# One joint turn of k and q, with k's remainder made in PSUM

## The chip, the cores and the metric

The kernel runs on one core of a Trainium2 chip. The metric is the device time of one execution in microseconds (us), as the median of several runs. The engines are TensorE (PE, with its weight loads as PEld), VectorE (DVE), ScalarE (ACT), GpSimd (POOL), and SyncE (SP), which issues all the transfers (DMA) of this program. Each engine works through its own instructions strictly in order and waits where one of them needs another engine's result.

## The reference

Attention over 8 batches, 12 heads, 448 tokens and 64 features, with q and k normalised by their root mean square; its output, 3584 rows of 768, goes through a feed-forward layer with w_in (768 x 2048), a squared ReLU scaled by s and shifted by b, and w_out (2048 x 768).

```python
def rmsnorm(x, g):
    rms = np.sqrt(np.mean(x * x, axis=-1, keepdims=True) + 1e-06)
    return x / rms * g
q_n, k_n = (rmsnorm(q, g_q), rmsnorm(k, g_k))
scores = scale * np.matmul(q_n, k_n.transpose(0, 1, 3, 2))
scores = scores - np.max(scores, axis=-1, keepdims=True)
attn = np.exp(scores)
attn = attn / (np.sum(attn, axis=-1, keepdims=True) + 1e-09)
out = np.matmul(attn, v)
...
h = x @ w_in
g = s * np.maximum(h, 0.0) ** 2 + b
return g @ w_out
```

## The kernel before

The 96 heads are worked on as 48 pairs, six pairs to a batch. The program is a list of slots, eight to a pair (four for each head j of the pair p), 384 in all, with a lead-in from slot -22 on. Nothing reorders the work: the loop writes each engine's instructions in the order of the slots, and `jobs` is a table that says which step is written in which slot. A step moved by one slot is moved past all that the slot holds, on each engine that it uses. In what follows a slot begins where its first product `st` (L451) begins.

In a slot s, PE computes a chunk of the transposed scores (`score_t`, L451 and L454), whatever is turned in this slot, a chunk of plain scores for a later pair (`score(s + AHEAD)`, L410), and the product with v of two slots earlier (`weigh`, L513). From slot 56 on six products of the feed-forward layer of the batch before are laid between these (`filler`, `ffn_in`, L208). DVE takes the maximum of the plain scores (`maximum`, L421); four of these make a row that a transfer puts beside q (`shift`). ACT takes the exponent (`exponent`).

All products are of two parts, so that they are exact enough: a value is rounded to a `hi` part, and what is left is the `lo` part. For a head of the first nine pairs (`NR`) the rows of k and q come as they lie in memory (`load_rows`), are normalised (`norm_rows`: ACT squares, DVE sums, POOL takes the power and multiplies), are turned by PE against the identity (`turn`, L278), and are split (`split_turned`): ACT rounds k and q out of PSUM (L286, L287, and q a second time into the other half of the partitions, L289), DVE makes the lo parts (L290 for k, L293 for q). `ka` holds k hi over k lo, `qa` q hi twice, `qb` q lo, and `kb` a copy of k hi that a transfer makes (`double_kb`, L398). Later pairs come turned from the host and use `norm`, `keep`, `spread`, `scale` and `split_kq`.

The weights w_in are 64-bit numbers in memory. They come in 24 pieces (`load_piece`, `convert`, L130 to L151), numbered 0 to 23 here: for each four instructions on DVE (L135, L138, L140, L143), two on ACT, and last one on POOL (L151), which writes the lo part `wil`. `PACE` says in which slots a piece begins; its hi part is written three slots later and its lo part four slots later. Block fc of the feed-forward layer needs pieces 6 * (fc // 4) to 6 * (fc // 4) + 5, in this order; block 12, the first that needs piece 23, is laid in slots 92 to 94. PSUM has eight banks, which a list hands out in turn (`psum`, `free`): a product waits until the bank that it is given has been read.

Of the kernel before, what the change touches and what calls it, by code (L numbers as in the profile page):

```python
# [9 lines left out]
F32 = mybir.dt.float32  # L10
# [17 lines left out]
AHEAD = 10  # L28
# [5 lines left out]
PACE = (-15, -10, *range(1, 61, 5), *range(59, 89, 3))  # L34
# [5 lines left out]
OUT = (92, *range(110, 141, 6), *(48 * b + i for b in range(3, 8) for i in range(14, 43, 7)))  # L40
# [3 lines left out]
def attention_then_relu2_ffn(  # L44
# [67 lines left out]
    warm = cpool.tile([P, 1], F32, name="warm")  # L112

# [128 lines left out]
    if True:  # L242
# [30 lines left out]
        def turn(p, j):  # L273
            raw = raws.pop((p, j))
            for t in range(2):
                tk, bank = psum(f"tk{p}_{j}_{t}")
                for c in range(NQ):
                    T.transpose(  # L278
                        tk[:D, c * QC : (c + 1) * QC], raw[:, t, c], ident[:QC, :QC]
                    )  # L280
                tks[p, j, t] = tk[:D, :SEQ], bank

        def split_turned(p, j):
            n, a = p % 2, slice(j * SEQ, (j + 1) * SEQ)
            (k, k_bank), (q, q_bank) = (tks.pop((p, j, t)) for t in range(2))
            S.copy(ka[n][:D, a], k)  # L286
            S.activation(qa[n][:D, a], q, AF.Copy, scale=gqk[:D])  # L287
            yield
            S.activation(qa[n][D:, a], q, AF.Copy, scale=gqk[:D])  # L289
            V.tensor_tensor(ka[n][D:, a], k, ka[n][:D, a].bitcast(F32), ALU.subtract)  # L290
# [364 lines left out]
        for p in range(NPAIR):  # L655
            s0 = W * p
            if p >= NR:
                at(s0 - 32, load, p)
                at(s0 - 28, norm, p)
                at(s0 - 24, keep, p)  # L660
            for j in range(2):
# [12 lines left out]
                at(s1 - 6, shift, p, j)  # L674
# [394 lines left out]
```

## Time and profile before

| | us |
|---|---|
| median of 3 runs | 1400.15 |
| lowest and highest run | 1399.1, 1400.77 |
| the profiled execution | 1402.48 |
| its span, from the first to the last instruction | 1400.7 |
| busy PE, DVE, ACT, POOL in it | 1379.6, 1038.5, 868.8, 1021.7 |
| start of slot 0, 56, 64 and 94 in the span | 24.22, 121.26, 144.56, 220.12 |

The page gives busy time by engine, the chain of waits, and groups of equal instructions with the mean time of one and the idle time of the engine ahead of them. "<-DVE nmx L421" names what ended the idle time. Since matmuls are pipelined, the time of one (0.37 us for the products of 448 columns) is longer than the distance from one to the next (0.2 us), so a busy PE may hide short waits; the distance between starts in the timeline is the better measure, and it is used throughout.

### The profile page before, as it was taken

What the parts mean: (1) busy time and instruction counts of PE and PEld (TensorE: products, weight loads), DVE (VectorE), ACT (ScalarE), POOL (GpSimd) and SP (SyncE); (2) the same over time, 40 slices, a digit from 0 to 9 for tenths busy, and PEclk for the clock granted to TensorE, in tenths of its full rate; (3) what the DMA queues carried; (4) which work ended last, traced back from release to release, by engine and by line L of the source; (5) the groups of instructions that cost most, each with busy time, mean ns of one, the idle gap of its engine ahead of it and who ended that gap; (6) DMA issues with size and microseconds to landing.
All of it is one profiled execution on the core that took longest, in us unless ns stands there. A gap on an engine that the chain in (4) does not pass through costs nothing. (4 is left out here: it accounts for less than half of the span.)

```text
span 1400.7 us, 22180 instructions
## 1 busy us (share of the span) xinstructions
PE 1379.6 (98%) x6976; PEld 1262.0 (90%) x6976; DVE 1038.5 (74%) x1603; ACT 868.8 (62%) x1658; POOL 1021.7 (73%) x940
## 2 busy tenths in 40 slices
PE   7999999999999999999999999999999999999998
PEld 5666888999999899999989989989999999999998
DVE  8999786888888778788788778565766665666655
ACT  5776666777777776776777777654544444444443
POOL 7687788777877787777787776267767777577763
PEclk8999999999999999999999999999999999999999
DMA  5566886777677677677677766354434333233331
GB/s 148 133 174 175 258 242 192 220 239 226 190 238 217 200 235 218 189 228 239 198 219 214 225 188 204 94 160 150 118 91 121 99 99 98 84 120 98 98 97 62
DMA packets 209253, 237.95 MB, mean 170 GB/s; under 512 B 72848, under 2 KB 187024, under 8 KB 209136
## 3 DMA queue, kind: packets, MB, share of 16 engines
q1 hardware_dynamic: 209136, 236.54, 57.6%
q8 instruction: 55, 0.90, 0.3%
q14 instruction: 62, 0.51, 0.1%
HBM read 178.00 MB, written 47.11 MB: 161 GB/s over the span
## 5 line engine op out<-in xcount | busy, mean ns | idle before, releaser
L208 PE MATMUL ph<-x,wih 128*128 128x448 f32 x1536 | 491.7, 366 | 0.5 <-DVE x L563 0.5
L848 PE MATMUL m<-t,gh 128*128 128x384 f32 x1568 | 399.3, 335 | 0.2
L208 PEld LDWEIGHTS ph<-x,wih 128*128 128x128 f32 x1536 | 288.6, 188 | 30.8 <-issue 6.7
L421 DVE TENSOR_REDUCE nmx<-sh 112x1 fp32r<-112x448 f32 x384 | 236.6, 618 | 85.3 <-PE sh L410 82.5
L208 PE MATMUL ph<-x,wil 128*128 128x448 f32 x768 | 294.0, 383 | 0.0
L848 PEld LDWEIGHTS m<-t,gh 128*128 128x128 f32 x1568 | 283.4, 188 | 1.0 <-DVE ot L863 0.9
L470 ACT ACTIVATE st<-st 128x448 f32<-128x448 f32 (+1 forms) x294 | 154.2, 524 | 192.9 <-PE st L454 189.9
L848 PE MATMUL m<-t,gl 128*128 128x384 f32 x784 | 262.6, 335 | 0.3 <-DVE gl L830 0.3
L829 ACT CAST gh<-g 128x896 fp32r<-128x896 f32 x112 | 105.4, 942 | 178.2 <-POOL g L819 178.2
L830 DVE TENSOR_TENSOR gl<-g,gh 128x896 fp32r<-128x896 f32 x112 | 127.7, 1141 | 107.2 <-ACT gh L829 107.2
L815 POOL TENSOR_TENSOR g<-g 128x256 f32<-128x256 f32 x112 | 94.6, 845 | 113.5 <-DVE g L814 113.5
L513 PE MATMUL av<-ah,vs 128*128 128x448 f32 x576 | 164.9, 367 | 0.8 <-DVE al L491 0.5
L451 PE MATMUL st<-qa,ka 128*128 128x448 f32 (+1 forms) x384 | 159.1, 414 | 4.1 <-DVE nmx L421 4.0
L208 PEld LDWEIGHTS ph<-x,wil 128*128 128x128 f32 x768 | 144.3, 188 | 17.9 <-issue 6.7
L478 ACT CAST ah<-st 128x448 fp32r<-128x448 f32 (+1 forms) x294 | 156.8, 533 | 1.3
L555 POOL TENSOR_TENSOR u<-uz,zb 64x448 f32<-64x448 f32 x96 | 126.7, 1320 | 42.1 <-DMA zb<-z_d 38.3
L410 PE MATMUL sh<-ka,qa 128*112 128x448 f32 x384 | 145.5, 382 | 3.6 <-DVE ka L290 1.8
L848 PEld LDWEIGHTS m<-t,gl 128*128 128x128 f32 x784 | 147.1, 188 | 0.6 <-DVE gl L830 0.6
L491 DVE TENSOR_TENSOR al<-st,ah 128x448 fp32r<-128x448 f32 x216 | 132.7, 614 | 18.7 <-ACT ah L478 15.8
L454 PE MATMUL st<-qb,kb 128*128 128x448 f32 (+1 forms) x384 | 140.4, 366 | 0.0
L394 POOL TENSOR_TENSOR ka<-kq,ka 64x448 fp32r<-64x448 f32 x78 | 95.5, 1224 | 57.0 <-ACT ka L391 52.3
L819 POOL TENSOR_TENSOR g<-g 128x256 f32<-128x256 f32 x112 | 125.9, 1124 | 0.0
(93 smaller groups left out, 2398.2 us busy)
## 6 DMA issues: line engine op xcount, KB each, us to landing
kq<-in_dram SPq DMA_DIRECT2D x78, 448.0 KB, 4.9
rb<-i_d SPq DMA_DIRECT2D x78, 448.0 KB, 5.9
r_d<-r SPq DMA_DIRECT2D x128, 224.0 KB, 3.1
raw<-in_dram SPq DMA_DIRECT2D x39, 448.0 KB, 5.1
raw<-r_d SPq DMA_DIRECT2D x64, 256.0 KB, 2.8
w64i<-in_dram SPq DMA_DIRECT2D x24, 512.0 KB, 4.7
w64o<-in_dram SPq DMA_DIRECT2D x32, 384.0 KB, 4.6
kb<-ka SPq DMA_DIRECT2D x96, 112.0 KB, 3.3
```

Of the source, the lines that this page charges most:

```text
L208: T.matmul(ph[:, :SEQ], w[:, cc, f0 : f0 + P], xs[b, cc][:, part, :], start=n == 0, stop=n == 3 * NCC - 1,)
L410: T.matmul(sh[:QC, :SEQ], qa[p % 2][:, a].rearrange("k (p c) -> k c p", c=NQ)[:, c], ka[p % 2][:, a], start=True, stop=True,)
L421: V.tensor_reduce(out=nmxs[p][:, c : c + 1], in_=sh[:QC, :SEQ], op=ALU.max, axis=AX.X, negate=True)
L451: T.matmul(st[:rows, :SEQ], ka[n][:, keys], qa[n][:, q], start=True, stop=False)
L454: T.matmul(st[:rows, :SEQ], kb[n][:, keys], qb[n][:, q], start=False, stop=True,)
L470: S.activation(st[:rows, :SEQ], st[:rows, :SEQ], AF.Exp)
L478: S.copy(ah[:rows], sts[i][0][:rows, :SEQ])
L491: V.tensor_tensor(al, st[:rows, :SEQ], ah[:rows].bitcast(F32), ALU.subtract)
L513: T.matmul(av[:, :SEQ], x, a, start=kc == 0 and m == 0, stop=kc == 3 and m == len(todo) - 1,)
L555: G.tensor_tensor(u[a], uzs.pop((p, j))[a], zb[a], ALU.mult)
L830: V.tensor_tensor(gl, g9[:, 1:8], gh.bitcast(F32), ALU.subtract)
L848: T.matmul(to, g[:, sa], w, start=m == 0 and n == 0, stop=m == NM - 1 and n == 2,)
```

## The change

`rows0` is laid so that k and q of a token lie side by side, and `turn` makes four turns of 128 columns (64 of k, 64 of q) into one PSUM bank where eight turns of 64 columns went into two. k comes out on partitions 0 to 63 and q on 64 to 127. From there `split_turned` differs by pair:

- q hi is written once by ACT, on partitions 64 to 127; its second copy is still written by ACT for pair 0, and by a transfer within SBUF (`move`) from pair 1 on.
- k lo is still made by DVE for pairs 0 and 1. From pair 2 on PE adds -k hi on the turned k: a product of `ka` with the constant `less`, a negative identity in its first 64 rows and columns and zero elsewhere, accumulated into the same bank; ACT then copies k lo out of PSUM a slot later.

With it go other numbers of the table: `AHEAD` is 9 (it was 10) and `shift` a slot later; `norm_rows` two slots earlier from pair 2 on; the last steps of the division (`invert`, `divide`) one or two slots later in batch 0, and `split_x` of its last pair one; `load` of pair 9 ten slots earlier; and `PACE`: piece 13 begins in slot 60 and no longer in 56, and the last, piece 23, in 90 and no longer in 86.

```diff
-AHEAD = 10
+AHEAD = 9
-PACE = (-15, -10, *range(1, 61, 5), *range(59, 89, 3))
+PACE = (-15, -10, *range(1, 56, 5), *range(60, 91, 3))
-OUT = (92, *range(110, 141, 6), ...
+OUT = (100, *range(110, 141, 6), ...
+    less = cpool.tile([P, P], F32R, name="less")
+    G.memset(less.bitcast(F32), 0.0)
+    S.activation(less[: P // 2, : P // 2], ident[: P // 2, : P // 2], AF.Copy, scale=-1.0)
...
         def turn(p, j):
             raw = raws.pop((p, j))
-            for t in range(2):
-                tk, bank = psum(f"tk{p}_{j}_{t}")
-                for c in range(NQ):
-                    T.transpose(
-                        tk[:D, c * QC : (c + 1) * QC], raw[:, t, c], ident[:QC, :QC]
-                    )
-                tks[p, j, t] = tk[:D, :SEQ], bank
+            tk, bank = psum(f"tk{p}_{j}")
+            for c in range(NQ):
+                T.matmul(
+                    tk[:, c * QC : (c + 1) * QC],
+                    raw[:, c].rearrange("p t d -> p (t d)"),
+                    ident[:QC, :QC],
+                    start=c == 0, stop=p < 2 and c == NQ - 1, is_transpose=True,
+                    skip_group_check=True,
+                )
+            tks[p, j] = tk, bank
 
         def split_turned(p, j):
             n, a = p % 2, slice(j * SEQ, (j + 1) * SEQ)
-            (k, k_bank), (q, q_bank) = (tks.pop((p, j, t)) for t in range(2))
+            tk, bank = tks.pop((p, j))
+            k, q = tk[:D, :SEQ], tk[D:, :SEQ]
             S.copy(ka[n][:D, a], k)
-            S.activation(qa[n][:D, a], q, AF.Copy, scale=gqk[:D])
+            S.activation(qa[n][D:, a], q, AF.Copy, scale=gqk[D:])
             yield
-            S.activation(qa[n][D:, a], q, AF.Copy, scale=gqk[:D])
-            V.tensor_tensor(ka[n][D:, a], k, ka[n][:D, a].bitcast(F32), ALU.subtract)
-            free.append(k_bank)
+            if p == 0:
+                S.activation(qa[n][:D, a], q, AF.Copy, scale=gqk[D:])
+            else:
+                move(qa[n][:D, a], qa[n][D:, a])
+            if p < 2:
+                V.tensor_tensor(ka[n][D:, a], k, ka[n][:D, a].bitcast(F32), ALU.subtract)
+            else:
+                T.matmul(
+                    tk[:, :SEQ], less, ka[n][:, a], start=False, stop=True, skip_group_check=True
+                )
             yield
+            if p >= 2:
+                S.copy(ka[n][D:, a], k)
             V.scalar_tensor_tensor(
...
-                at(s0 - 32, load, p)
+                at(s0 - (42 if p == NR else 32), load, p)
...
-                    at(s1 - 21, norm_rows, p, j)
+                    at(s1 - (21 if p < 2 else 23), norm_rows, p, j)
...
-                at(s1 - 6, shift, p, j)
+                at(s1 - 5, shift, p, j)
...
-            at(s0 + 13, invert, p)
-            at(s0 + 14, divide, p, 1)
-            at(s0 + 16, divide, p, 2)
-            at(s0 + 18, divide, p, 3)
+            first = p < NP
+            at(s0 + 13 + first, invert, p)
+            at(s0 + 14 + first, divide, p, 1)
+            at(s0 + 16 + first, divide, p, 2)
+            at(s0 + 18 + first + (p < NP - 1), divide, p, 3)
```

**PE, slots 10 to 12.** The turn of pair 3, head 0, in the kernel before (`sh` are the plain scores, `st` the transposed ones, `av` the product with v; four turns stand in a row that ends with x4).

```order
L451 MATMUL st10_613<-qa1_201,ka1_199 128x448
L454 MATMUL st10_613<-qb1_205,kb1_203 128x448
L278 MATMUL tk3_0_0_622<-ident_66,rows3_0_389 64x112 x4
L278 MATMUL tk3_0_1_627<-ident_66,rows3_0_389 64x112 x4
L410 MATMUL sh20_632<-ka0_198,qa0_200 112x448
L513 MATMUL av1_0_636<-e8_582,vf1_486 128x448
```

The same place in the changed kernel:

```order
L467 MATMUL st10_587<-qa1_204,ka1_202 128x448
L470 MATMUL st10_587<-qb1_208,kb1_206 128x448
L280 MATMUL tk3_0_597<-ident_66,rows3_0_378 128x112 x4
L426 MATMUL sh19_602<-ka0_201,qa0_203 112x448
L529 MATMUL av1_0_606<-e8_559,vf1_469 128x448
L467 MATMUL st11_608<-qa1_204,ka1_202 128x448
L470 MATMUL st11_608<-qb1_208,kb1_206 128x448
L426 MATMUL sh20_626<-ka0_201,qa0_203 112x448
L529 MATMUL av1_0_606<-e9_574,vf1_469 128x448
L467 MATMUL st12_634<-qa1_204,ka1_202 128x448
L470 MATMUL st12_634<-qb1_208,kb1_206 128x448
L303 MATMUL tk3_0_597<-ka1_202,less_74 128x448
```

Four turns have gone, and two slots later one product of 448 columns (L303) has come, which needs ACT's copy of k hi in `ka1`.

**SP, lead-in.** The transfers around the first `shift` (`qb0<-nmx0`) in the kernel before; `vf0` are the rows of v, `kb` the copies of k hi.

```order
L398 DMA qb0_204<-nmx0_321 1x112x4
L398 DMA kb0_202<-ka0_198 64x448
L324 DMA vf0_373<-in_3_dram 128x4x64 x2
L255 DMA rows3_0_389<-in_2_dram 112x512
L398 DMA qb0_204<-nmx0_321 1x112x4
```

The same place in the changed kernel:

```order
L414 DMA qb0_207<-nmx0_322 1x112x4
L340 DMA vf0_366<-in_3_dram 128x4x64 x2
L414 DMA qa1_204<-qa1_204 64x448
L258 DMA rows3_0_378<-in_2_dram 112x512
L414 DMA kb1_206<-ka1_202 64x448
L414 DMA qb0_207<-nmx0_322 1x112x4
```

The second copy of q hi (`qa1<-qa1`) now stands behind the shift and both loads of v; PE's plain score `sh8`, which stands ahead of the first `st0`, needs it.

**POOL, slots 91 to 94.** The end of the conversion of w_in (`wil3` is the last quarter of the lo part, `wai23` piece 23; `ri15` is the power of pair 15's norm, `vs0` a split of v), in the kernel before.

```order
L151 TENSOR_TENSOR wil3_1937<-wai23_2506,wih3_1936 128x512
L332 TENSOR_TENSOR v_rest_195<-vf11_2350,v_rest_195 128x2x64
L394 TENSOR_TENSOR ka1_199<-kq13_0_2408,ka1_199 64x448
L395 TENSOR_TENSOR qb1_205<-kq13_0_2408,qa1_201 64x448
L339 MEMSET vs0_2617 128x4x64 x2
L342 TENSOR_TENSOR vs0_2617<-vr12_2469,vs0_2617 128x4x2x64
L373 TENSOR_TENSOR kq13_1_2521<-kq13_1_2521,rb13_1_2523 128x448
L356 TENSOR_SCALAR ri15_2647<-ssq15_2614 128x14
L357 TENSOR_TENSOR ri15_2647<-ri15_2647,mhalf_71 128x14
L394 TENSOR_TENSOR ka1_199<-kq13_1_2521,ka1_199 64x448
```

The same place in the changed kernel:

```order
L410 TENSOR_TENSOR ka1_202<-kq13_0_2319,ka1_202 64x448
L411 TENSOR_TENSOR qb1_208<-kq13_0_2319,qa1_204 64x448
L355 MEMSET vs0_2535 128x4x64 x2
L358 TENSOR_TENSOR vs0_2535<-vr12_2376,vs0_2535 128x4x2x64
L389 TENSOR_TENSOR kq13_1_2432<-kq13_1_2432,rb13_1_2434 128x448
L372 TENSOR_SCALAR ri15_2565<-ssq15_2532 128x14
L373 TENSOR_TENSOR ri15_2565<-ri15_2565,mhalf_71 128x14
L154 TENSOR_TENSOR wil3_1960<-wai23_2520,wih3_1959 128x512
L410 TENSOR_TENSOR ka1_202<-kq13_1_2432,ka1_202 64x448
```

The lo part of piece 23 has moved from ahead of the split of v to behind pair 15's norm.

More of the change, by code (lines that the diff above doesn't have):

```diff
@@ L26 @@
 LAST = 15
-AHEAD = 10
+AHEAD = 9
 FIRST = -22
 FILL = (2, 2, 2)
-PACE = (-15, -10, *range(1, 61, 5), *range(59, 89, 3))
+PACE = (-15, -10, *range(1, 56, 5), *range(60, 91, 3))
 GAP = 2
 STEPS = {0: 2, 1: 3, 2: 4, 3: 5, 5: 6, 6: 7, 8: 8, 9: 9, 11: 10, 12: 11, 13: 12}
-OUT = (92, *range(110, 141, 6), *(48 * b + i for b in range(3, 8) for i in range(14, 43, 7)))
+OUT = (100, *range(110, 141, 6), *(48 * b + i for b in range(3, 8) for i in range(14, 43, 7)))
 @with_exitstack
@@ L253, in load_rows @@
             tag = f"{('kq', 'rb')[p % 2]}{j}"
-            raw = raws[p, j] = ap.tile([QC, 2, NQ, D], F32, tag=tag, name=f"rows{p}_{j}")
+            raw = raws[p, j] = ap.tile([QC, NQ, 2, D], F32, tag=tag, name=f"rows{p}_{j}")
             nc.sync.dma_start(raw, rows0[p, :, j])
         def norm_rows(p, j):
-            raw = raws[p, j].rearrange("p t c d -> p (t c) d")
+            raw = raws[p, j].rearrange("p c t d -> p (c t) d")
             n = 2 * NQ
@@ L681, in attention_then_relu2_ffn @@
                 at(s0 + 3, split_v_rest, p)
-            at(s0 + 13, invert, p)
-            at(s0 + 14, divide, p, 1)
-            at(s0 + 16, divide, p, 2)
-            at(s0 + 18, divide, p, 3)
+            first = p < NP
[3 more added lines that the diff above has]
+            at(s0 + 18 + first + (p < NP - 1), divide, p, 3)
         for b in range(B):
             for g in range(NP):
-                at(end(b + 1) - (2 if b < B - 1 else 4) + g, split_x, b, g)
+                at(end(b + 1) - (2 if b < B - 1 else 4) + g + (b == 0 and g == NP - 1), split_x, b, g)
         for s_ in (FIRST, FIRST + 3):
@@ L1052 @@
     rows0 = _np.stack([a.reshape(n, 2, 4, s // 4, d)[:9] for a in (k, q)], 2)
-    rows0 = rows0.transpose(0, 4, 1, 2, 3, 5)
+    rows0 = rows0.transpose(0, 4, 1, 3, 2, 5)
     laid = [kq, rows, rows0, vs, g] + [_np.asarray(inputs[x]) for x in _INS]
```

4 lines of the change are left out of this document (2 added, 2 removed).

## The prediction

> **What bounds the kernel now.** I read the page first, then the busy time by stretch, then the timelines of PE and of what it waits for.
>
> ```profile
> span 1400.7 us, 22180 instructions
> ...
> PE 1379.6 (98%) x6976; PEld 1262.0 (90%) x6976; DVE 1038.5 (74%) x1603; ACT 868.8 (62%) x1658; POOL 1021.7 (73%) x940
> ```
>
> PE is busy for 98% of the span, so taken whole, time is PE's work. The change touches the first 72 slots, so the share that counts is that of the stretches there (slots 0 to 56, 56 to 64, 64 to 72; the columns are the stretch, its length, the busy us of PE, weight loads, DVE, ACT and POOL with their instructions, the granted clock, and the transfers):
>
> ```profile
> 24.20:121.30 97.10, 91.70 (x390) 63.99 (x388) 90.59 (x159) 75.03 (x148) 71.70 (x79) 0.99 0.58 152
> 121.30:144.60 23.30, 21.45 (x91) 16.79 (x90) 20.60 (x33) 15.48 (x31) 16.50 (x15) 1.00 0.75 202
> 144.60:165.10 20.50, 20.50 (x90) 16.68 (x89) 13.86 (x24) 11.25 (x23) 14.98 (x14) 1.00 0.84 256
> ```
>
> From slot 64 on PE never rests: a change there counts only if it makes PE wait. In slots 0 to 56 DVE is busy for 90.6 of 97.1 us, and PE's busy time hides waits. What PE needs for itself shows in undisturbed slots, one with a turn (slot 10) and one without:
>
> ```profile
> 39.91 0.72 PE L451 MATMUL st<-qa,ka 128*128 128x448 f32 x1
> 40.47 0.36 PE L454 MATMUL st<-qb,kb 128*128 128x448 f32 x1
> 40.67 0.93 PE L278 MATMUL tk<-ident,rows 112*64 112x112 f32 x8
> 41.41 0.54 PE L410 MATMUL sh<-ka,qa 128*112 128x448 f32 x1
> ...
> 42.19 0.71 PE L451 MATMUL st<-qa,ka 128*128 128x448 f32 x1
> ...
> 43.55 0.71 PE L451 MATMUL st<-qa,ka 128*128 128x448 f32 x1
> ```
>
> A plain slot takes 43.55 - 42.19 = 1.36 us and one with a turn 42.19 - 39.91 = 2.28, so a turn costs 0.92. 56 slots with 14 turns are 56 x 1.36 + 14 x 0.92 = 89.0 us; the stretch took 97.1, so about 8.1 us are waits, and DVE ends the long ones:
>
> ```profile
> 103.36 1.09 DVE L353 TENSOR_REDUCE ssq<-raw 128x14 f32<-128x896 f32 x1 [1.46 <-ACT raw L348]
> 105.03 0.47 PE L451 MATMUL st<-qa,ka 128*128 128x448 f32 x1 [1.89 <-DVE nmx L421]
> 131.58 0.47 PE L451 MATMUL st<-qa,ka 128*128 128x448 f32 x1 [1.85 <-DVE nmx L421]
> ```
>
> The product waits for a bank that DVE's maximum still has to read. In slot 46 DVE itself was held by the square of pair 9, in slot 58 by its own queue.
>
> **The change, part by part.** *DVE in slots 0 to 56.* The groups of DVE in this stretch:
>
> ```profile
> L290 DVE TENSOR_TENSOR ka<-tk,ka 64x448 fp32r<-64x448 f32 x14 | 8.7, 618 | 1.0 <-ACT ka L286 0.6
> L138 DVE SCALAR_TENSOR_TENSOR bits<-w64i,bits 128x512 int32<-128x512 int32 x11 | 7.7, 699 | 0.4
> L140 DVE SCALAR_TENSOR_TENSOR bits<-w64i,bits 128x512 int32<-128x512 int32 x11 | 7.5, 686 | 0.0
> L135 DVE TENSOR_SCALAR bits<-w64i 128x512 int32<-128x512 int32 x11 | 7.5, 680 | 0.0
> L143 DVE SCALAR_TENSOR_TENSOR wai<-wih,bits 128x512 f32<-128x512 f32 x11 | 7.4, 668 | 0.0
> ```
>
> One of the 14 subtractions L290 here is pair 1's and stays; 13 go, 13 x 0.62 = 8.1 us (the 14th of pairs 2 to 8 lies behind slot 56). DVE is left with 90.6 - 8.1 = 82.5 us, less than PE's own 89. The early `load` of pair 9 also ends the 1.46 us that DVE lost in slot 46.
>
> *PE in the same slots.* Eight turns take 41.41 - 40.67 = 0.74 us, 0.093 each. No row has a turn of 128 columns. Two rows show what 64 more columns of weights cost:
>
> ```profile
> L454 PEld LDWEIGHTS st<-qb,kb 128*128 128x128 f32 x306 | 57.7, 189 | 13.7 <-issue 9.5
> L454 PEld LDWEIGHTS st<-qb,kb 128*64 128x64 f32 x78 | 10.5, 135 | 5.4
> ```
>
> That is 0.054 us. If it hides behind the moving columns, a turn still takes 0.093; if it is in series, 0.147. Four take 0.37 to 0.59; I take 0.5, nearer the series end, because turns follow each other with nothing to hide behind. The added product L303 has the shape of L454, which the next instruction follows 40.67 - 40.47 = 0.20 later. A turn then costs 0.92 - 0.74 + 0.50 + 0.20 = 0.88 (0.75 to 0.97), and PE's own work is 76.2 + 14 x 0.88 = 88.5 us (86.7 to 89.8). The joint turn pays for the added product and little more; the gain is DVE's.
>
> *What is queued behind L303.* It waits for ACT's copy of k hi, with the plain score and the product with v behind it on PE. In the case above ACT wrote k hi here:
>
> ```profile
> 43.65 0.51 ACT L286 CAST ka<-tk 64x448 fp32r<-64x448 f32 x1
> 44.06 0.63 ACT L287 ACTIVATE qa<-tk,gqk 64x448 fp32r<-64x448 f32 x1
> ...
> 44.30 0.36 PE L410 MATMUL sh<-ka,qa 128*112 128x448 f32 x1
> ```
>
> k hi is ready at 44.16, and PE stands at L303's place at 44.30: 0.14 us of slack, less than a weight load of 0.19. I charge 0.1 a turn, 1.4 us (0 to 0.5 a turn). The moved q hi is ready at 44.69; a transfer of the same size and kind, k hi into `kb`, lands in this stretch so:
>
> ```profile
> DMA to landing us min/median/max: 2.2/2.3/5.9
> ```
>
> That gives 47.0, or 48.3 if SP is held by the two loads of v ahead of it; the plain score that needs it stands four slots of 1.36 after the turn's slot, 42.19 + 4 x 1.36 + 0.4 = 48.0. Usually hidden.
>
> So the stretch goes from 97.1 to 88.5 + 1.4 + what remains of the 8.1 us of waits. DVE is still 82.5/89 = 93% loaded and its work comes in bursts (a piece of weights is 2.73 us), but a turn now holds one bank and not two, which lets DVE lag longer before PE notices. I leave 1.5 us: 91.4, **-5.7 us** (-2 if the waits stay but for slot 46, -9.5 if PE runs free at 0.75 a turn).
>
> *Slots 56 to 64* took 23.3, the next eight 20.5. Piece 13 leaves (0.680 + 0.699 + 0.686 + 0.668 = 2.73 us of DVE), and the last L290 too: the wait in slot 58 goes. The later division shortens the way of pair 5 from `divide` to the product that needs it by a slot; it fits. **-2.2** (0 to -2.8).
>
> *The end of the weights.* What piece 23 paid with is its slack. Before, its lo part lay four slots ahead of its use. Now it stands behind this on POOL, while PE needs it in slot 94 at the product `ph<-x,wil` of 221.94:
>
> ```profile
> 219.62 1.29 POOL L342 TENSOR_TENSOR vs<-vr,vs 128x512 fp32r<-128x512 f32 x1 [1.82 <-ACT vs L341]
> 220.87 1.15 POOL L373 TENSOR_TENSOR kq<-kq,rb 128x448 f32<-128x448 f32 x1
> 222.10 0.40 POOL L356 TENSOR_SCALAR ri<-ssq 128x14 f32<-128x14 f32 x1
> 222.59 3.30 POOL L357 TENSOR_TENSOR ri<-ri,mhalf 128x14 f32<-128x14 f32 x1
> ...
> 221.94 0.71 PE L208 MATMUL ph<-x,wil 128*128 128x448 f32 x1
> ...
> L151 POOL TENSOR_TENSOR wil<-wai,wih 128x512 fp32r<-128x512 f32 x24 | 30.9, 1286 | 5.3 <-ACT wih L149 4.9
> L357 POOL TENSOR_TENSOR ri<-ri,mhalf 128x14 f32<-128x14 f32 x39 | 103.1, 2644 | 3.2
> ```
>
> POOL is not late by a backlog that could shrink: it waited 1.82 us for ACT, which follows PE's slot 93. From 219.62 it needs 1.25 + 1.23 + 0.49, the power (2.64 on average, 3.30 here) and 1.29: the lo part is there at 226.5 to 227.2. PE, in order, waits 4.6 to 5.3 us, with all of the next slots behind it, in a stage where nothing is regained. **+4.8** (0 if POOL gets there otherwise, to +5.5).
>
> *The clock after it.* In the lead-in the granted clock goes down after stretches with little on PE:
>
> ```profile
> 8.31:11.72 3.41, 0.96 (x8) 0.72 (x8) 3.17 (x6) 1.99 (x4) 3.16 (x4) 1.00 0.18 53
> 11.72:15.13 3.41, 2.90 (x12) 2.34 (x12) 1.90 (x4) 3.08 (x6) 3.08 (x4) 0.50 0.77 226
> 15.13:18.55 3.42, 1.51 (x10) 1.08 (x10) 3.32 (x6) 0.63 (x1) 1.48 (x2) 1.00 0.21 66
> 18.55:21.96 3.41, 1.97 (x4) 0.68 (x3) 3.41 (x7) 1.95 (x4) 2.92 (x4) 0.50 0.44 145
> 21.96:25.37 3.41, 3.40 (x14) 3.05 (x15) 3.35 (x7) 2.61 (x6) 3.18 (x5) 0.50 0.47 103
> ```
>
> A stretch of 3.41 us with PE busy 0.96 or 1.51 us is followed by one at clock 0.50, and one that is nearly full (2.90, 3.40) lifts it again. A wait of 4.8 us leaves at least one such stretch under 45% busy wherever it falls, so a full stretch at half clock follows: 3.41 x 0.5 = 1.7 us, and up to 2.5 where part of another is at half clock too. **+1.8** (0 to +2.5).
>
> The Trainium skill (TensorE: Matmul & The Clock Gate, section "What's actually happening") says that the clock halves after at least one idle window of about 3.4 us in a free-running grid. The length agrees with the rows; but they show the drop after windows in which PE worked for 28% and 44%. By the rule alone a wait of 4.8 us would fill a whole window in only some 40% of its positions, and the sum would be 1.7 us better in the others.
>
> *The lead-in.* SP's transfers around slot 0 in the profile:
>
> ```profile
> 21.07 0.58 SPq L398 DMA_DIRECT2D qb<-nmx  x1
> ...
> 22.34 1.33 SPq L324 DMA_DIRECT2D vf<-in_dram  x2
> ...
> 24.22 0.57 PE L451 MATMUL st<-qa,ka 128*128 128x448 f32 x1
> ```
>
> The shift waits for the fourth maximum; behind it now come the two loads of v and only then the move of pair 1's q hi: 21.07 + 0.63 + 1.33 = 23.0, landed 2.3 later at 25.3, and the plain score ahead of `st0` needs it. DVE gets to the fourth maximum perhaps 0.7 earlier, since a plain score fewer stands ahead of the second turn. `st0` would begin at 25.0 against 24.22: **+0.8** (-0.6 if the move is not the last to arrive, to +2.5 if another stretch at half clock follows). ACT's and POOL's new constant lies in idle time ahead of the first turn. Behind slot 94 nothing but numbers of slots changes, at PE full: 0.
>
> The sum is -5.7 - 2.2 + 4.8 + 1.8 + 0.8 = -0.5 us against the profiled execution (1402.48, a span of 1400.7 and 1.8 around it), which is 2.3 above the median of the runs. Against the median that is **1399.6 us**.
>
> **The rivals.** *The weights arrive in time* (or POOL's power does not stand ahead of them): then +4.8 and +1.8 fall away and it is 1393. For it speaks only that POOL's spans are rough; against it, the order of POOL and four measured durations. *The first stage gains fully, or the clock stays up*: 2 to 4 us better, about 1396. For the first PE and DVE must mesh at all times, which the bursts speak against (0.12). For the second the clock must fall only after a stretch with PE wholly empty, which a wait of 4.8 us fills or not by where it falls; the rows of the lead-in speak against that (0.06). It is what the rule of the Trainium skill named above would give. *Slower: L303 waits.* The chain from `st` over the exponent and the copy of k hi back to PE is what a slot and a half takes; each turn in which ACT comes later than now holds PE. At 0.5 us a turn the 14 turns cost 7 and not 1.4, the stage gains 0.1, and it is 1405; from 0.3 a turn on (2.8 us more) the change is slower than now by more than the measurement can tell. For it speaks the slack of 0.14 us; against it, that ACT is busy for 75 of 97 us only, and that its added copy of k lo takes no longer than the L289 that it loses. *The change does not do what it says*: the order shows that it does.
>
> **How the numbers follow.** Forecast 0.50, with its own range 1396.5 to 1403; the weights in time 0.13; the full gain 0.18; L303 waits 0.19. About 0.2% (2.8 us) is what a measurement of this kernel can tell from no change: faster is under 1397.3, slower over 1403.0. Faster: 0.13 + 0.15 of the full gain + 0.08 of the forecast's lower end = 0.36. Slower: 0.16 of the last rival + 0.05 of the forecast's upper end = 0.21. The same: 0.43. The range 1393.5 to 1404.5 leaves out half of the first rival and the worse part of the last.
>
> **What would show it.** In the profile of the changed kernel: slot 56 begins about 5 us earlier, DVE's busy time between slots 0 and 56 is about 82 us, and the long waits of PE for a maximum in slots 46 and 58 are gone. PE waits once for POOL's `wil`, 4 to 5 us, some 212 us into the span, and a stretch at clock 0.50 follows. The first `st` begins near 25. Turns stand 0.10 to 0.15 apart. I am wrong if PE does not wait for `wil`, if the four turns take as long as the eight did, or if PE waits for ACT's `ka` in most turns.

## The result, and the profile after

The changed kernel takes 1418.24 us (median of 4 runs, 1415.64 to 1420.04); the kernel before, run beside it, 1400.46 (4 runs, 1399.1 to 1401.5). The ratio is 1.0126 with a 95% interval of 1.0105 to 1.0148, so the change makes the kernel slower by some 18 us. The forecast was 1399.6, its range ended at 1404.5, and it was wrong. The profiled execution took 1420.04 us; its page, with PE's share now 97 and not 98%:

```profile
span 1418.3 us, 22097 instructions
...
PE 1382.1 (97%) x6918; PEld 1263.0 (89%) x6918; DVE 1027.4 (72%) x1589; ACT 872.6 (62%) x1657; POOL 1018.7 (72%) x941
```

DVE has 14 instructions and 11 us less to do, as meant. Where the 17.6 us of span went shows by stretches, cut at the starts of the first `st` product of a slot (slot 0, 56 and so on) in the two traces:

| stretch | before | after | difference | forecast |
|---|---|---|---|---|
| ahead of slot 0 | 24.21 | 27.91 | +3.7 | +0.8 |
| slots 0 to 56 | 97.05 | 103.52 | +6.5 | -5.7 |
| slots 56 to 64 | 23.29 | 21.77 | -1.5 | -2.2 |
| slots 64 to 88 | 60.79 | 60.69 | -0.1 | 0 |
| slots 88 to 96 | 19.92 | 25.69 | +5.8 | +6.6 |
| slots 96 to 104 | 19.24 | 19.23 | 0 | 0 |
| slots 104 to 112 | 19.70 | 23.57 | +3.9 | 0 |
| slots 112 to 383 | 641.95 | 642.01 | +0.1 | 0 |
| behind slot 383 | 494.55 | 493.91 | -0.6 | 0 |

The busy time by stretch of the changed kernel, slots 0 to 56 and 56 to 64 (columns as in the prediction):

```profile
27.91:131.43 103.52, 92.34 (x346) 63.02 (x345) 81.74 (x140) 77.28 (x145) 67.08 (x76) 0.96 0.58 152
131.43:153.20 21.77, 21.66 (x91) 17.00 (x90) 15.53 (x28) 14.15 (x29) 13.63 (x13) 1.00 0.76 200
```

DVE is busy for 81.7 us, 8.9 less than before and what I expected, in a stage that is 6.5 us longer. So the relief came, and the stage is longer all the same. The view of what PE waited for (us in all, times, the longest) names who takes its place:

```profile
PE sh L426 <- DMA qa<-qa: 9.2, 3, 4.8
PE tk L280 <- POOL rows L274: 7.2, 4, 2.5
PE tk L303 <- ACT qa L294: 4.4, 9, 1.0
PE ph L211 <- POOL wil L154: 4.1, 1, 4.1
PE av L529 <- DVE al L507: 2.7, 2, 2.2
```

The second row lies ahead of slot 0, where 4.7 us of it were there before. The others are four new waits.

**L303 waits, but not for k hi.** A turn slot, two plain ones and the slot with the added product, on PE and on ACT:

```profile
38.07 0.72 PE L467 MATMUL st<-qa,ka 128*128 128x448 f32 x1
...
38.83 0.55 PE L280 MATMUL tk<-ident,rows 112*128 112x112 f32 x4
39.14 0.55 PE L426 MATMUL sh<-ka,qa 128*112 128x448 f32 x1
...
39.93 0.71 PE L467 MATMUL st<-qa,ka 128*128 128x448 f32 x1
...
41.29 0.71 PE L467 MATMUL st<-qa,ka 128*128 128x448 f32 x1
41.84 0.36 PE L470 MATMUL st<-qb,kb 128*128 128x448 f32 x1
42.59 0.47 PE L303 MATMUL tk<-ka,less 128*128 128x448 f32 x1 [0.39 <-ACT qa L294]
42.90 0.37 PE L426 MATMUL sh<-ka,qa 128*112 128x448 f32 x1
...
43.51 0.72 PE L467 MATMUL st<-qa,ka 128*128 128x448 f32 x1
```

```profile
40.95 0.54 ACT L482 ACTIVATE e<-st 128x448 f32<-128x448 f32 x1
41.39 0.51 ACT L293 CAST ka<-tk 64x448 fp32r<-64x448 f32 x1
41.91 0.63 ACT L294 ACTIVATE qa<-tk,gqk 64x448 fp32r<-64x448 f32 x1
```

The four turns take 39.14 - 38.83 = 0.31 us, less than I allowed. The slot with L303 takes 43.51 - 41.29 = 2.22, that is 0.86 over a plain one where I had 0.30. The product needs k hi, ready at 41.90, but it starts after q hi (42.54).

**The moved q hi is late.** SP's transfers ahead of slot 0 and around slot 23, and PE at the plain score that needs the move:

```profile
21.84 0.58 SPq L414 DMA_DIRECT2D qb<-nmx  x1
22.48 1.33 SPq L340 DMA_DIRECT2D vf<-in_dram  x2
23.92 0.57 SPq L414 DMA_DIRECT2D qa<-qa  x1
...
63.70 1.27 SPq L340 DMA_DIRECT2D vf<-in_dram  x2
65.03 0.61 SPq L133 DMA_DIRECT2D w64i<-in_dram  x1
65.75 0.51 SPq L414 DMA_DIRECT2D qa<-qa  x1
```

```profile
27.41 0.70 PE L426 MATMUL sh<-ka,qa 128*112 128x448 f32 x1 [4.79 <-DMA qa<-qa]
...
71.42 0.70 PE L426 MATMUL sh<-ka,qa 128*112 128x448 f32 x1 [2.77 <-DMA qa<-qa]
```

The DMA view of single issues has the landing: 5.5 us for the one at 65.75, which goes out behind 512 KB of weights.

```profile
qa<-qa SPq DMA_DIRECT2D x1, 112.0 KB, 5.5
```

Slot 23 takes 5.01 us for 1.36, and slots 43 and 55, where a head's plain scores begin as well, 3.09 and 3.17. The view puts the wait in slot 43 down to DVE's L269, but the score there starts at 108.40, 0.1 us after the move of that head landed (issued at 103.99, 4.3 us), and in e2 and e8 below, which have no moves, the slot takes 1.37 and 1.36.

**Slot 94** is the wait that I forecast, POOL in the order that I gave:

```profile
228.46 1.29 POOL L358 TENSOR_TENSOR vs<-vr,vs 128x512 fp32r<-128x512 f32 x1
229.71 1.13 POOL L389 TENSOR_TENSOR kq<-kq,rb 128x448 f32<-128x448 f32 x1
230.93 0.21 POOL L372 TENSOR_SCALAR ri<-ssq 128x14 f32<-128x14 f32 x1
231.22 2.59 POOL L373 TENSOR_TENSOR ri<-ri,mhalf 128x14 f32<-128x14 f32 x1
233.77 1.26 POOL L154 TENSOR_TENSOR wil<-wai,wih 128x512 fp32r<-128x512 f32 x1
...
235.09 0.74 PE L211 MATMUL ph<-x,wil 128*128 128x448 f32 x1 [4.08 <-POOL wil L154]
```

**Slot 106** I did not see. DVE is behind with the weights of w_out (L173) and with two instructions that take 1.6 us here and 0.89 and 0.97 on average, and the remainder L507 that PE needs comes after them:

```profile
263.53 0.55 DVE L173 SCALAR_TENSOR_TENSOR wao<-w64o,wao 128x384 f32<-128x384 f32 x1
264.00 1.58 DVE L390 SCALAR_TENSOR_TENSOR kq<-kq,gqk,rb 128x448 f32<-128x448 f32 x1
265.50 1.55 DVE L579 TENSOR_TENSOR x<-u,x 128x448 fp32r<-128x448 f32 x1
266.97 0.61 DVE L507 TENSOR_TENSOR al<-st,ah 128x448 fp32r<-128x448 f32 x1
...
267.73 0.64 PE L529 MATMUL av<-ah,vs 128*128 128x448 f32 x2 [2.21 <-DVE al L507]
```

Both of these waits, and the one in slot 23, are followed by a stretch at half clock:

```profile
70.96:74.37 3.41, 2.95 (x6) 2.03 (x7) 1.73 (x3) 0.00 (x0) 2.13 (x2) 0.50 0.11 16
231.40:234.80 3.40, 0.00 (x0) 0.00 (x0) 0.20 (x1) 0.00 (x0) 3.40 (x2) 1.00 0.58 154
234.80:238.20 3.40, 3.11 (x8) 2.57 (x9) 0.10 (x1) 1.22 (x3) 0.33 (x2) 0.50 0.56 186
265.50:268.90 3.40, 1.19 (x7) 1.08 (x7) 3.40 (x6) 0.91 (x3) 1.06 (x1) 1.00 1.02 377
268.90:272.30 3.40, 3.40 (x11) 2.90 (x10) 1.46 (x3) 2.35 (x5) 1.46 (x2) 0.50 0.51 180
```

### The profile page after: what moved, and what is told of

Read it like the earlier page. It is cut to its first block, busy times and chain, and to the rows that moved or that the text cites. A ratio compares the mean times of both kernels' runs of the same rounds, so it can differ in the third digit from the quotient of the medians.

```text
span 1418.3 us, 22097 instructions
## 1 busy us (share of the span) xinstructions
PE 1382.1 (97%) x6918; PEld 1263.0 (89%) x6918; DVE 1027.4 (72%) x1589; ACT 872.6 (62%) x1657; POOL 1018.7 (72%) x941
## 5 line engine op out<-in xcount | busy, mean ns | idle before, releaser
L832 POOL TENSOR_TENSOR g<-g 128x256 f32<-128x256 f32 x112 | 95.1, 849 | 113.6 <-DVE g L831 113.6
L507 DVE TENSOR_TENSOR al<-st,ah 128x448 fp32r<-128x448 f32 x216 | 132.7, 614 | 18.7 <-ACT ah L494 15.3
L426 PEld LDWEIGHTS sh<-ka,qa 128*112 128x112 f32 x384 | 107.9, 281 | 20.8 <-issue 5.6
```

The costliest lines, as they stand in the source:

```text
L426: T.matmul(sh[:QC, :SEQ], qa[p % 2][:, a].rearrange("k (p c) -> k c p", c=NQ)[:, c], ka[p % 2][:, a], start=True, stop=True,)
L507: V.tensor_tensor(al, st[:rows, :SEQ], ah[:rows].bitcast(F32), ALU.subtract)
```

## The experiments

All are edits of the changed kernel unless said otherwise; the table has them by name. Times are medians, the ratio is to the kernel before on the same chip with its interval, and the stretches are those of the table above, from one profiled execution each.

| run | us | ratio | slot 0 at | 0-56 | 56-64 | 88-96 | 104-112 |
|---|---|---|---|---|---|---|---|
| e1_half | 1421.02 | 1.0134 [1.0115, 1.0154] | 27.04 | 106.41 | 22.69 | 26.63 | 22.01 |
| e2_act | 1438.14 | 1.0252 [1.0230, 1.0274] | 23.99 | 125.23 | 24.13 | 26.66 | 22.01 |
| e3_pace | 1414.53 | 1.0095 [1.0066, 1.0124] | 28.21 | 105.24 | 24.22 | 19.92 | 20.17 |
| e4_out | 1418.90 | 1.0124 [1.0109, 1.0139] | 27.83 | 104.17 | 21.48 | 27.66 | 19.70 |
| e5_dvelo | 1413.96 | 1.0091 [1.0076, 1.0106] | 27.41 | 99.58 | 22.38 | 25.64 | 22.00 |
| e7_later | 1417.11 | 1.0114 [1.0097, 1.0131] | 28.26 | 100.62 | 22.33 | 25.48 | 23.55 |
| e8_later_act | 1413.40 | 1.0084 [1.0069, 1.0100] | 23.67 | 101.11 | 21.97 | 26.69 | 22.00 |
| e9_all | 1407.21 | 1.0038 [1.0025, 1.0051] | 23.62 | 101.04 | 25.37 | 19.92 | 19.69 |
| e10_sbuf | 1401.64 | 0.9999 [0.9990, 1.0009] | 23.82 | 96.14 | 22.43 | 19.92 | 19.70 |
| e11_mid | 1400.20 | 0.9993 [0.9984, 1.0003] | 23.81 | 96.28 | 21.92 | 19.92 | 19.70 |
| e12_joint | 1410.29 | 1.0067 [1.0052, 1.0082] | 23.74 | 103.46 | 23.72 | 19.92 | 19.70 |
| e13_turn | 1421.73 | 1.0155 [1.0140, 1.0170] | 24.92 | 114.36 | 23.58 | 19.92 | 19.71 |
| e14_lo | 1402.44 | 1.0010 [0.9999, 1.0020] | 23.37 | 97.96 | 22.07 | 19.91 | 19.71 |
| e15_ahead8 | 1400.20 | 0.9995 [0.9986, 1.0005] | 22.64 | 96.90 | 21.27 | 19.92 | 19.69 |
| e16_turn_sbuf | 1405.17 | 1.0038 [1.0024, 1.0051] | 22.93 | 99.54 | 23.58 | 19.91 | 19.69 |
| e17_lo_load | 1399.88 | 0.9994 [0.9985, 1.0003] | 23.38 | 95.20 | 21.70 | 19.92 | 19.70 |
| e18_load | 1398.17 | 0.9984 [0.9975, 0.9993] | 23.20 | 94.76 | 21.14 | 19.92 | 19.69 |

### Each of the four waits undone by itself

**The product on k's half only.**

```diff
-                    tk[:, :SEQ], less, ka[n][:, a], start=False, stop=True, skip_group_check=True
+                    k, less[:, :D], ka[n][:, a], start=False, stop=True, skip_group_check=True
```

> The added product L303 writes only k's 64 partitions of the bank (weights of 64 columns) in place of all 128; nothing else changes. Theory: in the changed kernel PE waits in L303 for ACT's copy of q hi (L294), because the product also rewrites q's half of the bank, and L294 ends 0.53 us after the copy of k hi (L293) that the product needs. Then the wait on L294 is gone, the slot two after each turn falls from about 2.2 us to 1.6 to 1.75, and the 14 turns give 6 to 8 us back: 1410 to 1412 us. Rival: ACT gets to the turn late as a whole; then L303 waits for L293 in the same slots, they stay above 2.0 us, and less than 2 us come back: 1416 to 1418.

My theory fell. L303 no longer touches q's half of the bank, and its group in slots 0 to 56 waits as before, for the same instruction:

```profile
L303 PE MATMUL tk<-ka,less 128*64 128x448 f32 x13 | 5.7, 441 | 5.1 <-ACT qa L294 5.1
```

The rival said L293 and is wrong too. What is left is that the wait is for the bank as a whole and not for the half.

**The second q hi by ACT.**

```diff
-            if p == 0:
+            if True:
                 S.activation(qa[n][:D, a], q, AF.Copy, scale=gqk[D:])
```

> The second copy of q hi is written by ACT again for all pairs (as the changed kernel does for pair 0), and not moved by SP; the product L303 is as in the changed kernel. Theory: the waits of PE for the moved copy fall away: slot 0 begins about 3 us earlier, slot 23 falls from 5.0 to about 1.4 us, and its half-clock stretch with it (1.7): 6 to 8 us less, 1410 to 1412 us. Rival: ACT's 13 added copies of about 0.5 us make ACT later for L303 and the exponents, at 0.3 us a turn another 4 us, and 1414 to 1416 us.

It is 20 us slower than the changed kernel, outside both. The move's own cost shows where I said: slot 0 begins at 23.99, and slot 23 takes 1.35. But L297 is one more reader of the bank ahead of L303, and PE waits for it although the product needs nothing from it:

```profile
PE tk L303 <- ACT qa L297: 28.1, 14, 2.6
```

That is 2 us a turn. With the run before, it says that the program orders the engines on a bank as a whole: whoever comes next waits for the last instruction of another engine there. (Each bank holds one tile of the program, so these runs do not tell an order by bank from an order by tile.)

**The table of the weight pieces, and that of w_out.**

```diff
-PACE = (-15, -10, *range(1, 56, 5), *range(60, 91, 3))
+PACE = (-15, -10, *range(1, 61, 5), *range(59, 89, 3))
```

> The table of the weight pieces is that of the kernel before (piece 13 back in the first stage, the last piece two slots earlier); nothing else changes. Theory: PE no longer waits for the lo part of piece 23 in slot 94 and no half-clock stretch follows: slots 88 to 96 fall from 25.7 to 19.9 us, 5.8 us less: 1412.4 us, because DVE has room in slots 46 to 60 for the piece that comes back. Rival: the piece makes DVE late in the first stage as in the kernel before; then slots 40 to 64 grow by 2 to 3 us and the net is 1414.5 to 1416 us.

```diff
-OUT = (100, *range(110, 141, 6), ...
+OUT = (92, *range(110, 141, 6), ...
```

> The first piece of w_out is converted from slot 92 on, as in the kernel before, and not from slot 100; nothing else changes. Theory: in the changed kernel its five steps on DVE fall on the slots in which batch 0's last x and batch 1's scores and score remainders need DVE, and PE waits 2.2 us for a remainder (L507) in slot 106, with a half-clock stretch behind it; with the piece at 92 both go, 3.9 us less: 1414.3 us. Rival: the wait comes from the other work that DVE has there (products beside POOL's), and slot 106 stays above 4 us: 1417 to 1419 us.

Each does at its place what the first theory said: slots 88 to 96 take 19.92 with the old pieces, slots 104 to 112 19.70 with the old w_out. The old pieces cost 2.4 us in slots 56 to 64 again (24.22 for 21.77) and 1.7 in the stage ahead of them, as the rival had it, and the net is its 1414.5, though its four runs lie far apart (1410.6 to 1419.7). The old pieces also take most of slot 106's loss away (20.17), so that this loss needs both new tables together. The 3.9 us of e4 do not show in its median: its slots 88 to 96 took 27.66 and not 25.69, and it is level with the changed kernel.

### The added product, its place and the move

> The joint turn, the moved q hi and all tables stay as in the changed kernel; only the lo part of k is again subtracted by DVE for all pairs, so the product L303 and ACT's copy L308 are gone. Theory 1 (the added product, with the wait in front of it, is what the first stage lost): the slot two after a turn falls from 2.2 us to 1.4, 13 x 0.86 = 11 us come back, DVE's 8 us of subtractions cost PE 2 to 5 us of waits in bursts: 1409 to 1412 us. Theory 2 (DVE's relief is worth what I predicted, 6 us or more): the waits for DVE's maximum return in slots 40 to 60 and the whole is 1413 to 1417 us.

```diff
-            if p < 2:
+            if True:
                 V.tensor_tensor(ka[n][D:, a], k, ka[n][:D, a].bitcast(F32), ALU.subtract)
...
-            if p >= 2:
-                S.copy(ka[n][D:, a], k)
```

1413.96: the slot two after a turn is at 1.36 again, yet the stage gains only 3.9 us of the 11. PE comes sooner to the moved q hi and waits longer there (6.00 us in slot 23, 4.64 in slot 55; 3.6 more than in the changed kernel over slots 23, 39, 43 and 55), and the 14 turn slots, with the subtraction back on DVE, take 3.1 more. No wait for DVE's maximum shows on PE in the stage, so the number of the second theory came without its reason. Next, L303 a slot later, as the changed kernel and then with ACT's second copy:

```diff
-            else:
+            yield
+            if p >= 2:
                 T.matmul(
...
-            yield
+                yield
             if p >= 2:
                 S.copy(ka[n][D:, a], k)
```

> As the changed kernel, but the product L303, and with it the copy of k lo and the subtraction for q lo, stand one slot later (two slots after the copies of k hi and q hi and not one). Theory 1: L303 waits because PE reaches it before ACT has read the bank twice; a slot later ACT is done, no wait is left, the product costs its 0.2 to 0.3 us, and 13 x 0.55 = 7 us come back: 1410 to 1412 us. Theory 2: PE has to wait for the ACT chain in any case; the wait moves to the plain score, which then needs k lo (L308) sooner after it is written: less than 3 us come back, 1415.5 us or more.

> As the run before it (L303 one slot later), and the second copy of q hi is written by ACT in place of the move on SP's queue, in the slot ahead of L303. Theory 1: slot 0 begins at about 24 us and not 27.9, the waits for the moved copy in slots 23, 39, 43 and 55 go (3.7 + 1.7 + 1.4 + 1.6 us) and a half-clock stretch with them, and L303 still finds ACT done: 1397 to 1402 us. Theory 2: ACT, 75% busy in this stage, has no room for 13 copies of 0.5 to 0.6 us; L303 waits for the second copy as it did in the run with ACT's copy alone (2 us a turn there), at 0.5 us a turn and more: 1404 to 1412 us.

In e7 L303 does not wait at all and costs 0.21 (slots of 1.57 beside 1.36), so its price in the changed kernel was its place. The stage gains only 2.9: the moves cost as much as before (5.60 us in slot 23, 3.47 in slot 39; 12.96 in slots 23, 39, 43 and 55 together for 13.02), and slots 7, 11, 15, 31 and others grow by 0.2 to 0.7, which the wait view puts in part (0.6 us) down to the k lo that is now a slot later. In e8 slot 0 is at 23.67 and no wait for the move is left, but L297 stands between: L303 waits 9.3 us for it. With the old tables on top:

> As the run before it (L303 one slot later, q hi copied by ACT), with the tables of the weight pieces and of w_out's first piece as in the kernel before. Theory 1: the four losses add up (0.86 a turn, the moved copy, slot 94 with its clock, slot 106), so this is 8 to 10 us below the run before it, 1389 to 1394 us, and DVE's relief of 8 us is then worth 6 to 10 us against the kernel before. Theory 2: the pieces that come back into the first stage load DVE so that PE waits for its maximum again; then it is 1396 to 1401 us, no better than the kernel before.

1407.21, above both: slots 88 to 96 and 104 to 112 are whole again, slots 56 to 64 take 25.4. L297's 9.3 us are still there, and the next run takes them away without moving an instruction. ACT's second copy reads the first in SBUF, not the bank:

```diff
-                S.activation(qa[n][:D, a], q, AF.Copy, scale=gqk[D:])
+                S.copy(qa[n][:D, a], qa[n][D:, a].bitcast(F32))
```

> L303 one slot later and the tables of the kernel before, as in the run called e9_all, but ACT's second copy of q hi reads the first copy in SBUF (qa) and not the PSUM bank. Theory 1 (PE in L303 waits for whatever ACT instruction last read the bank, needed or not): with no second reader the 12 waits for L297 (9.3 us) go, L303 costs 0.2 us, and it is 1397 to 1400 us. Theory 2 (ACT is simply full in these slots): PE waits for the copy in the plain score that needs it, or for k lo, and more than half of the 9.3 us stays: 1402 to 1406 us.

The group of the product from 24 to 130 us of the span (the 14th of e10 is the first one behind slot 56), first in e9, then in e10:

```profile
L304 PE MATMUL tk<-ka,less 128*128 128x448 f32 x13 | 6.2, 474 | 9.3 <-ACT qa L297 9.3
```

```profile
L304 PE MATMUL tk<-ka,less 128*128 128x448 f32 x14 | 5.2, 371 | 0.0
```

ACT does as many copies, at 0.56 for 0.63 us; only their source is another. The medians differ by 5.6 us; of the 7.7 between the two profiled executions, 4.9 lie in the stage and 2.9 in slots 56 to 64. The kernel is level with the one before. Then the last pieces two slots earlier than in the change:

```diff
-PACE = (-15, -10, *range(1, 61, 5), *range(59, 89, 3))
+PACE = (-15, -10, *range(1, 56, 5), *range(58, 89, 3))
```

> As e10_sbuf, but the pieces of w_in keep the changed kernel's first eleven places (1 to 51) and the last eleven stand two slots earlier than there (58, 61, ... 88). Theory 1: the lo part of piece 23 is on POOL ahead of the power of the norm and is there for slot 94, so slots 88 to 96 take 20 us, and with piece 13 still out of the first stage slots 56 to 64 take 22 us and not 25.4: 1393 to 1397 us, below the kernel before. Theory 2: with its last lo step in slot 92 the piece still lies behind POOL's other work and PE waits 2 to 4 us in slot 94 with a half-clock stretch: 1398 to 1401 us.

All four losses are gone (slots 56 to 64 take 21.9), and the repaired change takes 1400.20 us, ratio 0.9993: no difference from the kernel before. So the second question: why does the change bring nothing even then?

### What the two halves of the change do alone

The joint turn with k lo by DVE and ACT's copy, first with the old tables of the weights and the change's other tables, then with all tables of the kernel before, then with the second copy from SBUF as in e10:

> The joint turn alone, as far as it can stand alone: k lo by DVE for all pairs (no L303, no L308), the second copy of q hi by ACT, the tables of the weight pieces and of w_out as in the kernel before. Theory 1: four turns of 128 columns at 0.097 us take 0.37 us less than eight of 64, 14 x 0.37 = 5 us, of which DVE, as busy as in the kernel before, lets PE keep 1 to 3: 1398 to 1400 us. Theory 2: DVE is what bounds this stage without its relief, and the other moves of the change (scores nine slots ahead, norms earlier) cost as much: 1401 to 1404 us.

> The kernel before with the joint turn and nothing else of the change: all tables (scores ten slots ahead, norms, shift, pieces, divisions) are those before, ACT writes both copies of q hi, DVE subtracts k lo. Theory 1 (the shorter lookahead of nine slots made the run called e12_joint wait for DVE's maximum): the waits go, four turns in place of eight give 14 x 0.37 = 5 us less what DVE takes: 1396 to 1400 us. Theory 2 (the joint turn itself hurts: its one bank is held until both ACT and DVE have read k and q, and PE reaches DVE's bursts 0.37 us earlier a turn): 1402 to 1409 us.

> As e13_turn (the joint turn alone, all tables of the kernel before), but ACT's second copy of q hi reads the first one in SBUF and not the bank. Theory 1 (an instruction on a bank waits for the last one of another engine on that bank, also where it reads the other half): DVE's subtraction for k lo no longer waits for L297, DVE starts it some 0.6 to 1.2 us earlier a turn, and at least half of the 20 us comes back: 1402 to 1411 us. Theory 2 (DVE's bursts alone make PE wait): 1417 to 1422 us.

The joint turn by itself, with both copies of q hi read from the bank, is the worst part: +1.55% in e13, though PE has fewer turns. DVE's group L301 in slots 0 to 56 of e13 (the last figures are its idle time before them and what ended most of it), then the same group in e16:

```profile
L301 DVE TENSOR_TENSOR ka<-tk,ka 64x448 fp32r<-64x448 f32 x14 | 8.7, 618 | 15.9 <-ACT qa L297 15.7
```

```profile
L301 DVE TENSOR_TENSOR ka<-tk,ka 64x448 fp32r<-64x448 f32 x14 | 8.7, 618 | 2.6 <-ACT qa L294 2.3
```

DVE's subtraction reads k and k hi and nothing of q, and waits 15.7 us for ACT to have read q once more. In the kernel before k and q were in two banks, and the same subtraction waited 1.0. The maxima stand behind these subtractions on DVE, and PE waits for them, first in e13, then in e16:

```profile
PE sh L424 <- DVE nmx L435: 15.3, 11, 2.0
```

```profile
PE sh L424 <- DVE nmx L435: 1.4, 5, 0.3
```

One line, the source of that copy, gives 16.6 us back (1421.73 to 1405.17). Why e13 is 11 us slower than e12, where DVE's wait for L297 is 8.7 us and PE's for the maximum 7.8, lies in the other tables; I have not taken them apart. Nor is it shown why e16 is still 4.3 us above the kernel before: its stage is 2.5 us longer, though four turns for eight leave PE some 6 us less work there (14 x (0.74 - 0.31), an estimate from single slots).

The added product by itself, in the kernel before, with k in a bank of its own; then e11 with its plain scores a slot later (AHEAD 8, the shift at s1 - 4); then e14 with two table entries, and these two entries alone:

```diff
-            V.tensor_tensor(ka[n][D:, a], k, ka[n][:D, a].bitcast(F32), ALU.subtract)
-            free.append(k_bank)
+            if p < 2:
+                V.tensor_tensor(ka[n][D:, a], k, ka[n][:D, a].bitcast(F32), ALU.subtract)
+                free.append(k_bank)
+            else:
+                T.matmul(
+                    k, less[:, :D], ka[n][:, a], start=False, stop=True, skip_group_check=True
+                )
             yield
+            if p >= 2:
+                S.copy(ka[n][D:, a], k)
+                free.append(k_bank)
```

> The kernel before with the added product and nothing else: eight turns of 64 columns into two banks as before, k lo from pair 2 on by the product with the negative identity in k's own bank and ACT's copy of it; all tables as before. ACT has 13 copies more than before. Theory 1: PE gains a product of 0.2 us a turn (2.7 us), DVE loses 8.1 us of subtractions and with them most of the 8 us that PE waits in slots 0 to 58: 1395 to 1399 us. Theory 2: ACT's added copies and the wait of PE for k hi take what DVE gives: 1400 to 1406 us.

> As e11_mid, with the plain scores eight slots ahead and not nine, and the shift a slot later, so that k lo has one slot more to be ready. Theory 1: the plain score waits for k lo (1.8 us shown, and other slots of 1.8 to 2.9 us that show no wait) are the rest of what the stage loses; 2 to 4 us go: 1396 to 1398 us. Theory 2: the shorter lookahead brings the shift's transfer or DVE's maximum onto PE's path in exchange: 1400 to 1405 us.

```diff
-PACE = (-15, -10, *range(1, 61, 5), *range(59, 89, 3))
+PACE = (-15, -10, *range(1, 56, 5), *range(58, 89, 3))
...
-                at(s0 - 32, load, p)
+                at(s0 - (42 if p == NR else 32), load, p)
```

> As e14_lo (the added product alone, two banks a turn), with the load of pair 9's rows ten slots earlier, as the change has it, and the pieces of w_in at 1 to 51 and 58 to 88 as in e11_mid. Theory 1: the wait in slot 46 (4.9 us there, a plain turn slot is 2.24) goes and slots 56 to 64 keep 22 us: 3 to 5 us less than e14_lo, 1397 to 1400 us, and 2 us or more below the control that comes next. Theory 2: the gain is the load's and the table's alone, and the control is as fast.

> The control: the kernel before with the early load of pair 9 and the table of pieces of e17_lo_load, and nothing else. Theory 1: it gains the 3 us of slot 46 and about 1 us in slots 56 to 64, 1396.5 to 1398.5 us, and so stands within 1 us of the run with the product: DVE's 8 us were off the path. Theory 2: without DVE's relief the waits return elsewhere, 1399 to 1401 us.

With a bank of its own the product waits for nothing (its group x13 in e14: 5.1 us busy, 0.0 idle) and adds 0.21 a turn. The eight turns ahead of it also leave ACT some 0.4 us a turn more, so this run by itself does not show that the bank is the reason. The stage of e17, then that of its control e18:

```profile
23.38:118.57 95.19, 93.22 (x402) 65.14 (x401) 83.70 (x147) 83.03 (x161) 72.29 (x81) 1.00 0.56 156
```

```profile
23.20:117.96 94.76, 91.14 (x389) 63.82 (x388) 89.72 (x159) 74.97 (x148) 71.71 (x79) 1.00 0.58 155
```

The product takes 6 us from DVE and gives 8 to ACT and 2 to PE, and the stage is 0.4 us longer. By slots it is an even trade: the 14 slots with a turn take 34.2 us in e17 and 36.8 in e18, and the 13 slots with the product 20.6 and 17.8. So DVE's relief gives PE some 2.6 us, and the product takes 2.8. No run takes the subtractions away without putting the product in their place. In the joint turn the same trade is worth more: e9, with the product a slot later, takes 3.1 us less than e12, with the subtractions and the same tables, although PE waits 9.3 us there for L297. What the kernel before lost besides was in slots 46 to 64, with pair 9's late square and the piece that begins in slot 56; the two entries together take 2.3 us off slots 0 to 56 and 2.1 off slots 56 to 64. e18 is the fastest kernel of this study, 1398.17 us, ratio 0.9984 (0.9975 to 0.9993), some 2.7 us under the kernel before. e15 is level with e11 (1400.20 both), so the late k lo was not what was left of e11.

## Why the prediction was wrong, point by point

**What is queued behind L303** is the first step that failed. I charged 0.1 us a turn against k hi, ready 0.14 before PE's place. L303 waits for the last instruction of ACT on the bank, L294, which ends 0.64 us later (42.54 for 41.90). The slots two after a turn cost 10.5 us over plain ones in the changed trace, of which 13 x 0.20 is the product: 7.9 us, 0.6 a turn, where I had 1.4. The wait view books 4.4 of it as idle PE; the rest shows only in the distances between starts. I had a rival in this place at 0.5 a turn and gave it 0.19. Its size came and its reason did not: it had ACT come late with k hi, and k hi was there. The wait for q hi should have been the forecast, since the product writes all 128 partitions and the diff says so. That even the half would not have helped, only e1 shows.

**"Usually hidden"**, the moved q hi, is the second. The 2.3 us of landing that I took is the median of the move of k hi; the row's own 5.9 was the end that counted. The three moves that PE waited for in the stage landed in 5.5, 4.3 and 4.4 us and cost 3.7, 1.7 and 1.8 us in slots 23, 43 and 55, 7.2 together, the half clock behind slot 23's wait included as far as it falls into that slot. **The lead-in** is the same error: the move there landed in 3.4 us and 0.8 became 3.7; e2 and e8, without it, give 3.9 and 4.2 back.

**The turns** went the other way: four of 128 columns take 0.31 us and not 0.5, below my lower end of 0.37. PE's own work is 56 x 1.36 + 14 x 0.49 + 13 x 0.20 = 85.6 us and not 88.5. With 7.9 and 7.2 of waits that leaves 2.8 for what remains, where I had 1.5: together the 103.5 us of the stage.

**What the DVE relief is worth** had a wrong base as well. I read the 8.1 us between PE's own time and the stage as mostly DVE's and left 1.5. In the trace before, 6.8 of them lie in the 14 slots with a turn (38.7 us for 14 x 2.28) and 1.15 in slot 15 (2.51 for 1.36). The early load and the moved pieces take 2.3 of the stage away (e18), the relief itself some 2.6 in the slots with a turn (e17 against e18); 5.8 us of such waits stay in e18, and 3.5 in e17 beside the product's 13 x 0.21. That one bank for two would let DVE lag longer, as I argued, does not show either: in e13 PE waits 15.3 us for the maximum.

**The end of the weights and the clock after it**: the wait came in slot 94, 4.08 us for 4.8, with the half-clock stretch; the two slots together cost 5.8 for 6.6, and e3 takes exactly that away. The Trainium skill (TensorE: Matmul & The Clock Gate, section "What's actually happening") says that the clock halves after an idle window of about 3.4 us; the stretch 231.40 to 234.80 is empty and agrees. After slot 106 the clock fell behind a stretch with PE busy for 1.19 of 3.40 us, so "idle" there is not empty, as in the rows of the lead-in; and here it is ordinary products that PE worked on, where there it was mostly turns.

**"Behind slot 94 nothing but numbers of slots changes"** failed. The new OUT moves four steps of DVE and one of ACT (the expectation of e4 counts all five as DVE's) from slots 92 to 96 into 100 to 104, onto the remainders and x products of the next stage: 3.9 us in slots 106 and 107, which e4 takes away. A changed slot number is moved work, and I had counted it at nothing without naming what hides it.

**Slots 56 to 64** were right: -1.5 for -2.2.

## What to carry to other kernels

When two operands come to share a PSUM bank, list every instruction of every engine that touches it, in program order: in these runs each waited for the one before it on another engine, whether or not it used the same data, and that chain, not the number of instructions saved, was the price. Take further copies from SBUF instead of the bank. Before moving work off a busy engine, set what the move gives against what the replacement costs, slot by slot, in a run with that move alone: in a stage where DVE was busy for 89.7 of 94.8 us, 6 us less of its work gave PE 2.6 us, and the product in its place took them back.

## What the runs showed that I had not expected

Waits on a bank go by the whole bank. L303 on k's half waits 5.1 us for a read of q's half (e1); DVE's read of k waits 15.7 us for ACT's read of q (e13), a read behind a read; and in the changed kernel itself DVE's L309, which needs q and q hi, waits for ACT's read of k lo:

```profile
DVE qb L309 <- ACT ka L308: 14.5, 12, 2.0
```

The Trainium skill (PSUM — Partial Sum Buffer, section "PSUM bank collisions raise a hardware error") says that the compiler's scheduler adds a dependency between any two instructions on different engines that touch the same bank and the same quadrant of 32 partitions, reads and writes alike. The runs agree on reads. They are stricter on the place: k lies in partitions 0 to 63 and q in 64 to 127, no quadrant is shared, and the waits are there all the same. What the chip would do without them no run here shows.

A transposing product of 112 columns takes no longer with weights of 128 columns (0.31 us for four, 0.078 each) than with 64 (0.74 for eight, 0.093). And the transfer of one 112 KB tile within SBUF took 3.4 us ahead of slot 0 and 5.5, 4.3 and 4.4 where PE waited for it in the stage. All four went out directly behind loads of weights or of v; no run here separates this from what else was under way.
